# A first expert product by Strassen's seven block products instead of eight, in an fp32r attention and mixture-of-experts kernel

## The chip, the cores and the metric

One core of one Trainium2 chip runs the whole kernel in one launch. The metric is device time of the launch in microseconds (us); the time before is a median of three runs. Engines are written as in the profile: PE is the matrix engine, PEld its weight loads, DVE the vector engine, ACT the scalar engine, POOL GpSimd, SP the engine whose queue issues the DMAs.

## What is computed

An attention over 2 batches of 8 heads feeds a gated layer and then a mixture of four experts. The reference, cut to what the change touches (1152 tokens, model width 512, four experts of width 1024):

```python
def _moe_ref(x, w_a, w_b, w_out):
    a = x @ w_a
    b = x @ w_b
    return a * b @ w_out

def _moe2_ref(x, domain_probs, w1, w2):
    N, D = x.shape
    E = w1.shape[0]
    p = domain_probs / (domain_probs.sum(-1, keepdims=True) + 1e-09)
    out = np.zeros((N, D), dtype=np.float32)
    for e in range(E):
        h = np.maximum(x @ w1[e], 0.0)
        out += p[:, e:e + 1] * (h @ w2[e])
    return out
```

## The kernel before, in words

Every large product is made of three PE products: a number is kept as a high part rounded to fp32r and a low part that is the rest, and high by high, low-data by high-weight and high-data by low-weight are summed in PSUM. `mm3` (line 876) writes this for one output tile of 128 features by 1152 tokens: for each block of 128 in the contracted dimension, three part pairs, and for each of these three matmuls of 384 tokens (line 884), each with a weight load of its own.

There are four stages, one after the other. **Attention** fills the first 281 us. The **gated stage** makes twelve tiles `G[f]` out of `w_a` and `w_b`. The **w_out stage** sums the twelve `G[f]` into four tiles of `X`, one per 128 model features `d`: 12 x 9 = 108 matmuls each, then ACT writes the high part (line 955) and DVE the low part (line 956). `w_out` arrives as float64 and is decoded by `decode64` on ACT, DVE and POOL two half tiles ahead (`w_split`). The **expert stage** goes through four experts. For an expert, `h_chunk` (lines 974 to 985) makes eight feature tiles of `h`: 4 x 9 = 36 matmuls of 384 columns, then relu to a high part on ACT (line 980) and a low part on DVE (line 981). Between them `w_split` splits the next 1024 columns of `w1` or `w2` (ACT line 222, DVE line 223). Then, for nine token tiles of 128, 8 x 3 = 24 matmuls of 512 columns (line 1007) multiply `h` by `w2`, and DVE adds the weighted result to `acc` (lines 1012 and 1016). The first feature tile of the next expert is made before the last token tile. PSUM has two halves of three banks for feature tiles and banks 6 and 7 in turn for token tiles.

All engines run in the order in which the kernel is written, each in its own order, with semaphores between them. Weights are loaded by SP in items of 1 MB into two buffers `stg`; an item's load is issued when an older item has been split.

Of the kernel before, what the change touches and what calls it, by code (L numbers as in the profile page):

```python
# [20 lines left out]
NT = B * SQ  # L21
# [70 lines left out]
def kernel(  # L92
# [16 lines left out]
    wsp = ctx.enter_context(tc.tile_pool(name="wsp", bufs=2))  # L109
# [7 lines left out]
    X = xpool.tile([128, 2, KC, NT], F32R, name="X")  # L117

# [9 lines left out]
    for e in range(E):  # L128
        at = len(items)
        for kind, u in (("w1", 0), ("w1", 1), ("w2", 0), ("w1", 2), ("w2", 1), ("w1", 3), ("w2", 2), ("w2", 3)):  # L130
            splits.append((kind, (e, u), at + u // 2 * 2 + (kind == "w2"), (u % 2) * 1024, 1024))
        items += [src[e, i].bitcast(I32) for i in range(2) for src in (w1, w2)]
# [13 lines left out]
    def decode64(raw, hi, lo, n):  # L146
        parts = []
        for i in range(2):
            cs = slice(i * n // 2, (i + 1) * n // 2)
            v, c, t = (pools["tmp"].tile([128, pools["n"]], F32, tag=f"{x}{i}", name=x)[:, :n // 2] for x in "vct")  # L150
            low, high = raw[:, cs, 0].bitcast(U32), raw[:, cs, 1].bitcast(U32)
            parts.append((low, high, v, v.bitcast(U32), c, c.bitcast(U32), t, hi[:, cs], lo[:, cs]))
# [43 lines left out]
    def w_split():  # L196
        for _ in w_split_steps():
            pass

    def w_split_steps():  # L200
        i = nxt["split"]
        if i >= len(splits):
            return
        nxt["split"] += 1
        kind, idx, item, off, n = splits[i]
        if kind == "w2":
            pool = pools["w2"]
        elif kind == "w1":
            pool = wsp
        else:  # L210
            pool = pools["w3"] if i % 3 == 2 else wsp
        t = pool.tile([128, 2, 1024], F32R, tag="w", name="w")
        s = staged[item]
        if kind in ("ab", "o"):
            raw = s.rearrange("p (n w) -> p n w", w=2)
            for o in range(0, n, 2 * pools["n"]):
                cs = slice(o, min(n, o + 2 * pools["n"]))
                yield from decode64(raw[:, cs, :], t[:, 0, cs], t[:, 1, cs], cs.stop - o)
            last = True
        else:  # L220
            s = s[:, off:off + n].bitcast(F32)
            nc.scalar.activation(out=t[:, 0, :n], in_=s, func=AF.Copy)  # L222
            nc.vector.tensor_tensor(  # L223
                out=t[:, 1, :n], in0=s, in1=t[:, 0, :n].bitcast(F32), op=ALU.subtract
            )
            last = off > 0
        W[kind, idx] = t
        if last:
            del staged[item]
            w_dma()  # L230

    with tc.manual_schedule():
# [11 lines left out]
        pools["tmp"] = att.enter_context(tc.tile_pool(name="tmp", bufs=1))  # L244
# [646 lines left out]

        g_x = ExitStack()
        g_p = g_x.enter_context(tc.tile_pool(name="g", bufs=1))
        a_sp = g_x.enter_context(tc.tile_pool(name="asb", bufs=1))
        pools["n"] = 512
        pools["tmp"] = g_x.enter_context(tc.tile_pool(name="tmp2", bufs=1))
        pools["w3"] = g_x.enter_context(tc.tile_pool(name="w3", bufs=1))
        G = [g_p.tile([128, 2, NT], F32R, name=f"G{f}") for f in range(NF)]
        xs = lambda kc: X[:, :, kc, :]

        def gv(t):
            return t.rearrange("p (n c) -> p n c", c=TOK)
# [4 lines left out]
        def gate(f, groups):  # L907
            asb = a_sp.tile([128, NT], F32, tag="a", name="asb")
# [25 lines left out]
        for f in range(1, NF):  # L934
            if f == STOP:
                g_x.close()
# [9 lines left out]
        for d in range(KC):  # L946
            px2 = psum("ps", 0, NTC, 2)
            for hf in range(2):
                w = W.pop(("o", (d, hf)))
                if (d, hf) != (KC - 1, 0):  # L950
                    w_split()
                hs = range(hf * NF // 2, (hf + 1) * NF // 2)
                mm3(banks(px2), lambda f: w, lambda f: (f % (NF // 2)) * 128, lambda f: G[f],
                    hs, range(NTC), 0, NF - 1)
            nc.scalar.activation(out=gv(X[:, 0, d, :]), in_=px2[:, :, :TOK], func=AF.Copy)
            nc.vector.tensor_tensor(
                out=gv(X[:, 1, d, :]), in0=px2[:, :, :TOK],
                in1=gv(X[:, 0, d, :].bitcast(F32)), op=ALU.subtract,
            )
        g_x.close()  # L960

        pools["w2"] = ctx.enter_context(tc.tile_pool(name="w2p", bufs=4))
        h_p = ctx.enter_context(tc.tile_pool(name="h", bufs=9))
        acc_p = ctx.enter_context(tc.tile_pool(name="acc", bufs=1))
        acc = acc_p.tile([128, NTT, DM], F32, name="acc")

        nc.sync.dma_start(out=p_sb, in_=probs)
        nc.vector.tensor_reduce(out=p_sum, in_=p_sb, axis=AX.X, op=ALU.add)
        nc.vector.tensor_scalar(out=p_sum, in0=p_sum, scalar1=1e-9, scalar2=None, op0=ALU.add)
        nc.vector.reciprocal(out=p_rec, in_=p_sum)  # L970
        for e in range(E):
            nc.vector.tensor_tensor(out=p_n[:, :, e], in0=p_sb[:, :, e], in1=p_rec, op=ALU.mult)

        def h_chunk(e, f):
            w = W["w1", (e, f // 2)]
            ph = psum("ps", 0, NTC, 2)
            mm3(banks(ph), lambda kc: w, lambda kc: ((f % 2) * KC + kc) * 128, xs,
                range(KC), range(NTC), 0, KC - 1)
            hs = h_p.tile([128, 2, NT], F32R, tag="h", name="hs")
            nc.scalar.activation(out=gv(hs[:, 0, :]), in_=ph[:, :, :TOK], func=AF.Relu)  # L980
            nc.vector.scalar_tensor_tensor(  # L981
                out=gv(hs[:, 1, :]), in0=ph[:, :, :TOK], scalar=0.0,
                in1=gv(hs[:, 0, :].bitcast(F32)), op0=ALU.max, op1=ALU.subtract,
            )
            return hs

        hs = [None] * NFE
        for e in range(E):
            for f in range(NFE):
                if hs[f] is None:  # L990
                    hs[f] = h_chunk(e, f)
                if f < 7:
                    w_split()
            cur, hs = hs, [None] * NFE
            w2s = [W.pop(("w2", (e, u))) for u in range(4)]
            for tt in range(NTT):
                if tt == 1 and e + 1 < E:
                    w_split()
                if tt == NTT - 1 and e + 1 < E:
                    hs[0] = h_chunk(e + 1, 0)  # L1000
                po = psum("po", 6, 1, 2)[:, 0, :]
                ts = slice(tt * 128, (tt + 1) * 128)
                for f in range(NFE):
# [7 lines left out]
                if e == 0:  # L1011
                    nc.vector.tensor_scalar(
                        out=acc[:, tt, :], in0=po, scalar1=p_n[:, tt, 0:1], scalar2=None, op0=ALU.mult
                    )
                else:
                    nc.vector.scalar_tensor_tensor(  # L1016
                        out=acc[:, tt, :], in0=po, scalar=p_n[:, tt, e:e + 1], in1=acc[:, tt, :],
                        op0=ALU.mult, op1=ALU.add,
                    )
                if e == E - 1:  # L1020
                    nc.sync.dma_start(out=out[ts, :], in_=acc[:, tt, :])
# [43 lines left out]
```

## Time and profile before

| what | us |
|---|---|
| median of three runs (906.33, 906.46, 908.34) | 906.46 |
| span of the profiled execution, first to last instruction | 907.1 |
| PE busy | 896.2 (99%) |
| DVE busy | 459.4 (51%) |
| ACT busy | 270.8 (30%) |
| POOL busy | 71.6 (8%) |

The profiled execution is known by its span, 907.1 us; its own time on the clock of the runs is not marked among the three, and the span lies 0.6 us above their median. The profile counts a PE matmul from its start to its modelled end, so matmuls overlap and the mean duration of one is longer than the step from one to the next. The step is what a stage costs, and it is had from a merged row of the chain of waits (time over count) or from the starts of rows in the timeline.

### The profile page before, as it was taken

To read this page: it belongs to the slowest core of one execution; us is meant where nothing else is said; L and a number is where in the kernel's file an instruction comes from. 1 tells how busy PE (TensorE), PEld (TensorE's weight loads), DVE (VectorE), ACT (ScalarE), POOL (GpSimd) and SP (SyncE) were. 2 spreads that over 40 slices of the span, in tenths; PEclk is the share of its full clock that TensorE was granted. 3 is DMA by queue.
4 is the path that set the end of the run, shared out by engine and by line. 5 is a ranking of instruction groups with operands and counts; after the bars stand their busy time and mean duration, and the time that the engine had idled before them with its cause. 6 is when DMAs were issued, how large, how long until landed. Compare 5 with 4: busy or idle time off the path is not lost.

```text
span 907.1 us, 11505 instructions
## 1 busy us (share of the span) xinstructions
PE 896.2 (99%) x4709; PEld 818.5 (90%) x4709; DVE 459.4 (51%) x793; ACT 270.8 (30%) x395; POOL 71.6 (8%) x42
## 2 busy tenths in 40 slices
PE   8999999999999999999999999999999999999998
PEld 6787888888889999999999999889988998899986
DVE  5875766776605888988784243114321242114311
ACT  4444455545453333333321222002300221003200
POOL 6000000000000222222221000000000000000000
PEclk9999999999999999999999999999999999999999
DMA  7567676766440222212212112001300121011011
GB/s 181 128 152 197 154 187 162 180 158 151 120 111 1 94 93 93 85 49 79 91 70 94 47 54 86 1 0 47 135 5 1 47 94 47 1 43 51 4 54 47
DMA packets 49385, 76.99 MB, mean 85 GB/s; under 512 B 32496, under 2 KB 36084, under 8 KB 45748
## 3 DMA queue, kind: packets, MB, share of 16 engines
q1 hardware_dynamic: 49332, 76.25, 29.7%
q8 instruction: 37, 0.61, 0.3%
q14 instruction: 16, 0.13, 0.0%
HBM read 51.96 MB, written 2.39 MB: 60 GB/s over the span
## 4 chain that ended last, share of the span: by engine, by line
PE 93%; DVE 3%; DMA 2%; SPq 1%; ACT 1%; issue 0%; DVEq 0%; ACTq 0%
PE PS L884 44%; PE PS L1007 22%; PE PS L543 14%; PE PS L418 5%; PE PS L528 4%; PE PS L533 4%; PE PS L508 1%; DMA kq<-in_kq_dram 1%; SPq L390 1%; DMA QH<-QH 0%; DVE R L872 0%; SPq L144 0%; DVE v L168 0%; DVE m L433 0%; PE PS L499 0%
## 5 line engine op out<-in xcount | busy, mean ns | idle before, releaser
L884 PE MATMUL PS<-X,w 128*128 128x384 f32 x2016 | 351.7, 334 | 0.6 <-ACT asb L910 0.5
L884 PEld LDWEIGHTS PS<-X,w 128*128 128x128 f32 x2016 | 349.7, 188 | 1.8 <-ACT asb L910 1.3
L1007 PE MATMUL PS<-w,hs 128*128 128x512 f32 x864 | 197.3, 389 | 0.0
L1007 PEld LDWEIGHTS PS<-w,hs 128*128 128x128 f32 x864 | 162.1, 188 | 33.4
L543 PE MATMUL PS<-e,VF 128*128 128x288 f32 x540 | 150.6, 410 | 0.7 <-ACT U L564 0.3
L433 DVE TENSOR_REDUCE m<-PS 128x1 f32<-128x384 f32 (+1 forms) x213 | 112.0, 553 | 61.2 <-PE PS L418 57.6
L980 ACT ACTIVATE hs<-PS 128x1152 fp32r<-128x1152 f32 x32 | 36.3, 1135 | 281.3 <-PE PS L884 281.3
L538 ACT ACTIVATE e<-PS 128x576 f32<-128x576 f32 x135 | 84.5, 649 | 113.8 <-PE PS L533 113.1
L543 PEld LDWEIGHTS PS<-e,VF 128*128 128x128 f32 x540 | 98.8, 190 | 20.3 <-ACT U L564 0.9
L981 DVE SCALAR_TENSOR_TENSOR hs<-PS,hs 128x1152 fp32r<-128x1152 f32 x32 | 43.4, 1357 | 134.3 <-ACT hs L980 134.3
L188 POOL TENSOR_TENSOR t<-v,w 128x512 f32<-128x512 f32 (+2 forms) x22 | 56.4, 2564 | 408.1 <-ACT w L178 408.1
L1016 DVE SCALAR_TENSOR_TENSOR acc<-PS,p_n,acc 128x512 f32<-128x512 f32 x27 | 20.3, 751 | 115.7 <-PE PS L1007 115.7
L418 PE MATMUL PS<-kh,QB 128*128 128x384 f32 x189 | 73.1, 427 | 2.9 <-DVE m L433 2.6
L884 PE MATMUL PS<-G,w 128*128 128x384 f32 x432 | 75.0, 334 | 0.0
L884 PEld LDWEIGHTS PS<-G,w 128*128 128x128 f32 x432 | 74.9, 188 | 0.0
L528 PE MATMUL PS<-QH,A 128*128 128x288 f32 x270 | 65.5, 324 | 0.0
L533 PE MATMUL PS<-QL,B 128*128 128x288 f32 x270 | 57.6, 295 | 0.0
L528 PEld LDWEIGHTS PS<-QH,A 128*128 128x128 f32 x270 | 48.3, 190 | 5.7
L418 PEld LDWEIGHTS PS<-kh,QB 128*128 128x128 f32 x189 | 35.1, 190 | 11.4 <-DVE m L433 5.7
L533 PEld LDWEIGHTS PS<-QL,B 128*128 128x128 f32 x270 | 43.6, 189 | 0.0
L223 DVE TENSOR_TENSOR w<-stg,w 128x1024 fp32r<-128x1024 f32 x32 | 38.9, 1215 | 8.1 <-ACT w L222 8.1
L193 DVE TENSOR_TENSOR w<-t,c 128x512 fp32r<-128x512 f32 (+2 forms) x44 | 39.3, 931 | 1.0
(84 smaller groups left out, 482.6 us busy)
## 6 DMA issues: line engine op xcount, KB each, us to landing
stg<-in_w_dram SPq DMA_DIRECT2D x16, 1024.0 KB
stg<-in_wab_dram SPq DMA_DIRECT2D x12, 1024.0 KB
stg<-in_wout_dram SPq DMA_DIRECT2D x8, 768.0 KB
VF<-in_vo_dram SPq DMA_DIRECT2D x16, 288.0 KB
A<-kl SPq DMA_DIRECT2D x15, 288.0 KB
q<-in_kq_dram SPq DMA_DIRECT2D x7, 576.0 KB
kq<-in_kq_dram SPq DMA_DIRECT2D x21, 192.0 KB
A<-kh SPq DMA_DIRECT2D x14, 288.0 KB
```

The source lines that it names most:

```text
L188: nc.gpsimd.tensor_tensor(out=t, in0=v, in1=h.bitcast(F32), op=ALU.subtract)
L193: nc.vector.tensor_tensor(out=l, in0=t, in1=c, op=ALU.add)
L223: nc.vector.tensor_tensor(out=t[:, 1, :n], in0=s, in1=t[:, 0, :n].bitcast(F32), op=ALU.subtract)
L418: nc.tensor.matmul(out=out[:lhs.shape[1]], lhsT=lhs, rhs=rhs, start=True, stop=True)
L433: nc.vector.tensor_reduce(out=max_slot(h, qi)[:, r:r + 1], in_=mx[:n_q(h, qi)], axis=AX.X, op=ALU.max)
L528: nc.tensor.matmul(out=st[:, c, :HQ], lhsT=At[i][:, ks], rhs=QHt[i][:, c * HQ:(c + 1) * HQ], start=True, stop=False,)
L533: nc.tensor.matmul(out=st[:, c, :HQ], lhsT=Bt[i][:, ks], rhs=QLt[i][:, c * HQ:(c + 1) * HQ], start=False, stop=True,)
L538: nc.scalar.activation(out=e, in_=st[:, :, :HQ], func=AF.Exp, scale=1.0 / 16.0)
L543: nc.tensor.matmul(out=PS[:, c, :HQ], lhsT=VFt[h % 2][:, t, :], rhs=e[:, c, :], start=(t == 0), stop=(t == KT - 1),)
L884: nc.tensor.matmul(out=ps[n], lhsT=wt(kc)[:, wi, w0:w0 + 128], rhs=src(kc)[:, xi, n * TOK:(n + 1) * TOK], start=(kc == first and i == 0), ...
L981: nc.vector.scalar_tensor_tensor(out=gv(hs[:, 1, :]), in0=ph[:, :, :TOK], scalar=0.0, in1=gv(hs[:, 0, :].bitcast(F32)), op0=ALU.max, op1=A ...
L1007: nc.tensor.matmul(out=po, lhsT=cur[f][:, hi, ts], rhs=wv[:, wi, cs], start=(f == 0 and i == 0), stop=(f == NFE - 1 and i == 2),)
```

## The change

The first expert product is rewritten with the form of Strassen's identity that needs seven block products. The contracted dimension and the features are taken in blocks of 128 as 2 x 2 blocks: a pair `p` of feature tiles (f0, f1) is one side, the four blocks of 128 model features the other, and the tokens are cut into halves T1 and T2 of 576. For each of 16 pairs, `h_pair` runs seven products (`product`), each over two blocks of 128, three part pairs and two matmuls of 288 tokens: 12 matmuls, into one of three pairs of PSUM banks. The sums of weight blocks (S1 to S4) are made per pair on DVE (`prep_w1`). The sums of token blocks (T1 to T4) do not depend on the expert and are made once, in the w_out stage, out of PSUM; that stage's last tile (d = 3) is for this cut into two token halves (`o_last`) of 72 matmuls of 288 columns. The seven results are added up by DVE in SBUF tiles `v1` to `v4`, and relu then makes high and low parts out of these. The product with `w2` runs once per two pairs, that is eight times over nine token tiles of 12 matmuls, where before it ran four times over nine tiles of 24; DVE adds into `acc` 72 times, before 36. Of the token tiles those of T2 come first. Buffers of the gated stage (`GT`) are reused for sums, weights and `h`. The decode in the gated stage keeps its difference in the buffer of its input.

The diff, cut to its core:

```diff
-    wsp = ctx.enter_context(tc.tile_pool(name="wsp", bufs=2))
+    wsp = ctx.enter_context(tc.tile_pool(name="wsp", bufs=1))
...
+        def tmp_g(i):
+            v, c = (tmp4[:, 2 * i + j, :] for j in range(2))
+            return v, c, v
...
+        def prep_w1(p, tmp, then=True):
+            k, q = divmod(p, 2)
+            s = f32(staged[len(splits) + 2 * k][:, q * 1024:(q + 1) * 1024])
+            a11, a12, a21, a22 = (s[:, i * 256:(i + 1) * 256] for i in range(4))
...
+            tt(tmp[:, 0], a11, a21, ALU.subtract)
+            tt(a21, a21, a22, ALU.add)
+            tt(tmp[:, 1], a21, a11, ALU.subtract)
+            act(t[:, :, 0], s)
+            yield
+            tt(t[:, :, 1], s, f32(t[:, :, 0]), ALU.subtract)
+            tt(a12, a12, tmp[:, 1], ALU.subtract)
+            yield
+            s23, s4 = pair_sets.get(p, sets[q])
+            hl = s23.rearrange("p h (j n) -> p h j n", j=2)
+            act(hl[:, 0], tmp)
+            act(s4[:, 0], a12)
+            tt(hl[:, 1], tmp, f32(hl[:, 0]), ALU.subtract)
+            tt(s4[:, 1], a12, f32(s4[:, 0]), ALU.subtract)
...
+        def prep_w2(p):
...
+            act(t[:, :, 0], s)
+            tt(t[:, :, 1], s, f32(t[:, :, 0]), ALU.subtract)
...
+        o_last(1)
+        tt(hv(b12[1]), pd[1], hv(b12[1]), ALU.subtract)
+        tt(hv(t1[1]), pd[1], hv(t1[1]), ALU.subtract)
+        split(opT["T2"][0], t2)
+        split(opT["T2"][1], t1[1])
+        split(opT["T3"][0], b12[0])
+        split(opT["T3"][1], b12[1])
+        split_ps(X[:, :, 3, T2], pd[1])
+        run(prep_w1(1, w_tmp))
+        o_last(0)
+        tt(hv(t1[1]), pd[0], hv(t1[1]), ALU.subtract)
+        split_ps(X[:, :, 3, T1], pd[0])
+        split(opT["T4"][0], t4)
+        split(opT["T4"][1], t1[1])
...
+                for j, (wi, xi) in enumerate(((0, 0), (0, 1), (1, 0))):
+                    for n in range(2):
+                        nc.tensor.matmul(
+                            out=q[:, n], lhsT=lhs[:, wi, i * 128:(i + 1) * 128],
+                            rhs=rhs[:, xi, n * HC:(n + 1) * HC],
+                            start=(i == 0 and j == 0), stop=(i == 1 and j == 2),
+                        )
+            return q
...
+        def h_pair(p, work):
+            f0, f1 = 2 * (p % 2), 2 * (p % 2) + 1
+            v1, v2, v3, v4 = (hv(v) for v in vs)
+            act(v1, product(p, "A11", "B11"))
+            tt(v2, v1, product(p, "S2", "T2"), ALU.add)
+            tt(v3, v2, product(p, "S3", "T3"), ALU.add)
+            next(work, None)
+            q = product(p, "S1", "T1")
+            tt(v2, v2, q, ALU.add)
+            tt(v4, v3, q, ALU.add)
+            relu_hi(f1, T2, v4)
+            tt(v1, v1, product(p, "A12", "B21"), ALU.add)
+            relu_hi(f0, T1, v1)
+            relu_lo(f1, T2, v4)
+            tt(v2, v2, product(p, "S4", "B22"), ALU.add)
+            relu_hi(f0, T2, v2)
+            relu_lo(f0, T1, v1)
+            next(work, None)
+            relu_lo(f0, T2, v2)
+            tt(v3, v3, product(p, "A22", "T4"), ALU.add)
+            relu_hi(f1, T1, v3)
+            relu_lo(f1, T1, v3)
+            next(work, None)
...
-                for f in range(NFE):
-                    wv = w2s[f // 2]
-                    cs = slice((f % 2) * DM, (f % 2 + 1) * DM)
+                for f in range(4):
...
-                            out=po, lhsT=cur[f][:, hi, ts], rhs=wv[:, wi, cs],
-                            start=(f == 0 and i == 0), stop=(f == NFE - 1 and i == 2),
+                            out=po, lhsT=hs[f][:, hi, ts], rhs=w2s[f // 2][:, f % 2, wi],
+                            start=(f == 0 and i == 0), stop=(f == 3 and i == 2),
```

The built program has 1344 matmuls of `product`, 144 of `o_last`, 1188 of 384 columns in the gated stage and the first three tiles of the w_out stage, and 864 of 512 columns; attention is the same, instruction for instruction. Before, there are 2448 of 384 columns (1152 of them in `h_chunk`, 432 in the w_out stage) and 864 of 512. How the order of the instructions moved is shown at three places.

DVE in the expert stage of before, between two feature tiles (`hs` is a feature tile, `w` a split weight tile):

```order
L981 SCALAR_TENSOR_TENSOR hs_4974<-PS_108,hs_4974 128x1152
L223 TENSOR_TENSOR w_4977<-stg_4625,w_4977 128x1024
L981 SCALAR_TENSOR_TENSOR hs_5016<-PS_108,hs_5016 128x1152
L223 TENSOR_TENSOR w_5019<-stg_4936,w_5019 128x1024
L981 SCALAR_TENSOR_TENSOR hs_5058<-PS_108,hs_5058 128x1152
```

And DVE of the change in the second pair of a group, where every odd pair has the low part of a `w2` tile (row 3) in its chain:

```order
L948 TENSOR_TENSOR v2_4275<-v1_4274,PS_110 128x576
L948 TENSOR_TENSOR v3_4276<-v2_4275,PS_110 128x576
L948 TENSOR_TENSOR GT_2391<-stg_4772,GT_2391 128x2x512
L948 TENSOR_TENSOR v2_4275<-v2_4275,PS_110 128x576
L948 TENSOR_TENSOR v4_4277<-v3_4276,PS_110 128x576
L948 TENSOR_TENSOR v1_4274<-v1_4274,PS_110 128x576
L1137 SCALAR_TENSOR_TENSOR GT_2391<-v4_4277,GT_2391 128x576
L948 TENSOR_TENSOR v2_4275<-v2_4275,PS_110 128x576
L1137 SCALAR_TENSOR_TENSOR GT_2391<-v1_4274,GT_2391 128x576
L1137 SCALAR_TENSOR_TENSOR GT_2391<-v2_4275,GT_2391 128x576
L948 TENSOR_TENSOR v3_4276<-v3_4276,PS_110 128x576
L1137 SCALAR_TENSOR_TENSOR GT_2391<-v3_4276,GT_2391 128x576
```

One DVE pass over a finished feature tile has become eleven passes over half rows for two tiles, seven of which read PSUM and free it.

PE at the end of a group's products and in the first token tile behind them, of the change (a wait in brackets names the engine waited for; the `GT` on the left of a 512-column row is `h`):

```order
L1126 MATMUL PS_110<-X_73,GT_2391 128x288 [waits DVE_49]
L1126 MATMUL PS_110<-X_73,GT_2391 128x288 x11
L1126 MATMUL PS_110<-GT_2391 128x288 [waits DVE_49]
L1126 MATMUL PS_110<-GT_2391 128x288 x11
L1198 MATMUL PS_110<-GT_2391 128x512 x6
L1198 MATMUL PS_110<-GT_2391 128x512 [waits Activation_49]
L1198 MATMUL PS_110<-GT_2391 128x512
L1198 MATMUL PS_110<-GT_2391 128x512 [waits DVE_49]
L1198 MATMUL PS_110<-GT_2391 128x512 x15
```

The token tile's seventh matmul waits for ACT and its ninth for DVE: these read the T2 half of the odd pair's f0, the last one of that half to be finished.

DVE at the change's last tile of the w_out stage (`asb`, `x0` and `x1` hold token sums; the rows begin when the T2 half has been summed in PSUM):

```order
L948 TENSOR_TENSOR asb_2403<-PS_110,asb_2403 128x576
L948 TENSOR_TENSOR x0_2404<-PS_110,x0_2404 128x576
L948 TENSOR_TENSOR GT_2391<-x1_2405,GT_2391 128x576
L948 TENSOR_TENSOR GT_2391<-x0_2404,GT_2391 128x576
L948 TENSOR_TENSOR GT_2391<-asb_2403,GT_2391 128x576 x2
L948 TENSOR_TENSOR X_73<-PS_110,X_73 128x576
L948 TENSOR_TENSOR w_tmp_4083<-stg_3935 128x256
L948 TENSOR_TENSOR stg_3935<-stg_3935 128x256
L948 TENSOR_TENSOR w_tmp_4083<-stg_3935 128x256
L948 TENSOR_TENSOR GT_2391<-stg_3935,GT_2391 128x2x512
L948 TENSOR_TENSOR stg_3935<-stg_3935,w_tmp_4083 128x256
L948 TENSOR_TENSOR GT_2391<-w_tmp_4083,GT_2391 128x512
```

Before, one row (line 956) stands in this place; now the token sums and the second pair's weight sums are made there, beside the T1 half's matmuls on PE.

## Rows read from the trace of the kernel before

**Rows 1.** The page's span, PE's busy time, and the granted clock in 40 slices.

```profile
span 907.1 us, 11505 instructions
PE 896.2 (99%) x4709; PEld 818.5 (90%) x4709; DVE 459.4 (51%) x793; ACT 270.8 (30%) x395; POOL 71.6 (8%) x42
...
PEclk9999999999999999999999999999999999999999
```

**Rows 2.** Busy time by stretch: us, each engine's busy us (instructions), granted clock, DMA.

```profile
400.00:450.00 50.00, 50.00 (x290) 50.00 (x289) 43.38 (x81) 15.87 (x26) 13.34 (x5) 1.00 0.21 66
...
550.00:600.00 50.00, 50.00 (x232) 42.61 (x231) 10.23 (x11) 4.16 (x4) 0.00 (x0) 1.00 0.06 22
```

**Rows 3.** Chain that ended last: start us, us, engine, line, instructions merged; expert stage.

```profile
557.30 43.56 PE PS L1007 x192
...
612.61 43.70 PE PS L884 x252
...
854.34 49.02 PE PS L1007 x216
```

**Rows 4.** PE's timeline in attention: start us, us from first start to last end.

```profile
183.78 0.42 PE L533 MATMUL PS<-QL,B 128*128 128x288 f32 x2
184.04 0.42 PE L528 MATMUL PS<-QH,A 128*128 128x288 f32 x2
184.31 0.43 PE L533 MATMUL PS<-QL,B 128*128 128x288 f32 x2
184.57 0.41 PE L543 MATMUL PS<-e,VF 128*128 128x288 f32 x1
```

**Rows 5.** Line 884 by instruction: duration ns min/median/max, first and last start, forms.

```profile
L884 PEld LDWEIGHTS PS<-G,w x432: 187/188/188, 432.2 to 506.9; 128*128 128x128 f32 x144
L884 PE MATMUL PS<-G,w x432: 334/334/334, 432.3 to 507.0; 128*128 128x384 f32 x144
```

**Rows 6.** The weight loads' timeline in the same piece of attention.

```profile
183.65 0.32 PEld L533 LDWEIGHTS PS<-QL,B 128*128 128x128 f32 x2
183.91 0.32 PEld L528 LDWEIGHTS PS<-QH,A 128*128 128x128 f32 x2
184.18 0.32 PEld L533 LDWEIGHTS PS<-QL,B 128*128 128x128 f32 x2
```

**Rows 7.** Groups of DVE and ACT instructions: busy us, mean ns, idle before and its releaser.

```profile
L981 DVE SCALAR_TENSOR_TENSOR hs<-PS,hs 128x1152 fp32r<-128x1152 f32 x32 | 43.4, 1357 | 134.3 <-ACT hs L980 134.3
L223 DVE TENSOR_TENSOR w<-stg,w 128x1024 fp32r<-128x1024 f32 x32 | 38.9, 1215 | 8.1 <-ACT w L222 8.1
L1016 DVE SCALAR_TENSOR_TENSOR acc<-PS,p_n,acc 128x512 f32<-128x512 f32 x27 | 20.3, 751 | 115.7 <-PE PS L1007 115.7
L184 DVE SCALAR_TENSOR_TENSOR c<-stg,c 128x512 f32<-128x512 uint32 x20 | 12.8, 682 | 0.0
L340 DVE TENSOR_TENSOR qs<-q 128x576 f32<-128x576 f32 x7 | 5.3, 753 | 0.0
L597 DVE TENSOR_TENSOR U<-U,R 128x288 f32<-128x288 f32 x16 | 7.2, 452 | 5.7 <-DMA R<-rd 5.5
L538 ACT ACTIVATE e<-PS 128x576 f32<-128x576 f32 x135 | 84.5, 649 | 113.8 <-PE PS L533 113.1
L222 ACT ACTIVATE w<-stg 128x1024 fp32r<-128x1024 f32 x32 | 33.7, 1053 | 8.4 <-PE PS L884 8.4
```

**Rows 8.** Timeline of DVE and ACT in the w_out stage, third tile.

```profile
472.41 0.62 DVE L157 TENSOR_SCALAR c<-c 128x384 f32<-128x384 f32 x2
...
485.01 1.65 DVE L193 TENSOR_TENSOR w<-t,c 128x384 fp32r<-128x384 f32 x2
...
488.69 1.14 ACT L955 ACTIVATE X<-PS 128x1152 fp32r<-128x1152 f32 x1 [5.14 <-PE PS L884]
```

**Rows 9.** Busy time in the stretch in which one weight item of 1 MB lands.

```profile
517.30:523.00 5.70, 5.70 (x35) 5.70 (x34) 2.00 (x3) 2.08 (x2) 0.00 (x0) 1.00 0.48 184
```

**Rows 10.** Timeline of the end: the last addition on DVE and the last store.

```profile
903.38 0.75 DVE L1016 SCALAR_TENSOR_TENSOR acc<-PS,p_n,acc 128x512 f32<-128x512 f32 x1 [4.69 <-PE PS L1007]
904.15 0.33 SPq L1021 DMA_DIRECT2D out_dram<-acc  x1
```

More of the change, by code (lines that the diff above doesn't have):

```diff
@@ L117 @@
     X = xpool.tile([128, 2, KC, NT], F32R, name="X")
+    WA = [wsp.tile([128, 2, 1024], F32R, name=f"WA{i}") for i in range(2)]
     items = []
@@ L128 @@
     for e in range(E):
[L129 to L132, printed above, removed]
+        for i in range(2):
+            items += [w1[e, i].bitcast(I32), w2[e, i].bitcast(I32)]
     nxt = {"dma": 0, "split": 0}
@@ L205, in w_split_steps @@
         kind, idx, item, off, n = splits[i]
[L206 to L226, printed above, removed]
+        t = WA[i % 3]
+        raw = staged[item].rearrange("p (n w) -> p n w", w=2)
+        for o in range(0, n, 2 * pools["n"]):
+            cs = slice(o, min(n, o + 2 * pools["n"]))
+            yield from decode64(raw[:, cs, :], t[:, 0, cs], t[:, 1, cs], cs.stop - o)
         W[kind, idx] = t
-        if last:
-            del staged[item]
-            w_dma()
+        del staged[item]
+        w_dma()
     with tc.manual_schedule():
@@ L944, with act, tt, f32 @@
             gate(f, [(pa[:, :, :TOK], pb[:, :, :TOK], 0, NT)])
-        for d in range(KC):
+        HT = NT // 2
+        HC = HT // 2
+        SP = HT - TOK
+        T1, T2 = slice(0, HT), slice(HT, NT)
+        def act(out, in_, func=AF.Copy):
+            nc.scalar.activation(out=out, in_=in_, func=func)
+        def tt(out, in0, in1, op):
+            nc.vector.tensor_tensor(out=out, in0=in0, in1=in1, op=op)
+        def f32(t):
+            return t.bitcast(F32)
+        def split(t, v):
+            act(t[:, 0], v)
+            tt(t[:, 1], v, f32(t[:, 0]), ALU.subtract)
@@ new lines, in o_w @@
+        def o_w(d, hf):
+            w = W.pop(("o", (d, hf)))
+            if d < KC - 1:
+                w_split()
+            return w
+        b12 = [asb[:, i * HT:(i + 1) * HT] for i in range(2)]
+        t1 = [b12[1], t1b]
+        opT = {n: [] for n in ("T2", "T3", "T4")}
+        for i in range(2):
+            opT["T2"].append(GT[:, i, :, T2])
+            opT["T3"].append(GT[:, 2 + i, :, T2])
+            opT["T4"].append(GT[:, i, :, T1])
+        sets = [
+            (GT[:, 4, :, HT:HT + 512], GT[:, 5, :, HT:HT + 256]),
+            (GT[:, 2, :, 0:512], GT[:, 3, :, 0:256]),
+        ]
@@ new lines, in prep_w2, with run @@
+        def prep_w2(p):
+            k, q = divmod(p, 2)
+            s = f32(staged[len(splits) + 2 * k + 1][:, q * 1024:(q + 1) * 1024])
+            s = s.rearrange("p (j n) -> p j n", j=2)
+            t = W["w2", p] = slot_of(4 * k + 2 + q)
+            act(t[:, :, 0], s)
+            tt(t[:, :, 1], s, f32(t[:, :, 0]), ALU.subtract)
+            if q == 1:
+                del staged[len(splits) + 2 * k + 1]
+                w_dma()
+        def run(steps):
+            for _ in steps:
+                pass
@@ L955 @@
[L955 to L958, printed above, removed]
-            )
[L960 to L985, printed above, removed]
@@ L987 @@
-        hs = [None] * NFE
-        for e in range(E):
-            for f in range(NFE):
[L990 to L1000, printed above, removed]
+                    fs, range(NTC), 0, NF - 1)
@@ new lines, with o_last @@
+        d_x.close()
+        s_p = g_x.enter_context(tc.tile_pool(name="s0", bufs=1))
+        pair_sets[0] = [s_p.tile([128, 2, n], F32R, name=f"s{n}") for n in (512, 256)]
+        w_tmp = s_p.tile([128, 512], F32, name="w_tmp")
+        run(prep_w1(0, w_tmp))
+        w = [o_w(KC - 1, hf) for hf in range(2)]
+        pd = [PS[:, 6:8, :HC], PS[:, 4:6, :HC]]
+        def o_last(half):
+            at = half * HT
+            for f in range(NF):
+                for i, (wi, xi) in enumerate(((0, 0), (0, 1), (1, 0))):
+                    for n in range(2):
+                        nc.tensor.matmul(
+                            out=pd[half][:, n],
+                            lhsT=w[f // (NF // 2)][:, wi, (f % (NF // 2)) * 128:(f % (NF // 2) + 1) * 128],
+                            rhs=G[f][:, xi, at + n * HC:at + (n + 1) * HC],
+                            start=(f == 0 and i == 0), stop=(f == NF - 1 and i == 2),
+                        )
@@ new lines @@
+        run(prep_w1(1, w_tmp))
[4 more added lines that the diff above has]
+        split(opT["T4"][1], t1[1])
+        a_x.close()
+        v_p = ctx.enter_context(tc.tile_pool(name="v", bufs=1, side="right"))
+        s_tmp, *vs = (v_p.tile([128, n], F32, name=f"v{i}") for i, n in enumerate((512, HT, HT, HT, HT)))
+        turn["q"] = 0
+        Q = [PS[:, 2 * i:2 * i + 2, :HC] for i in range(3)]
@@ new lines, in product @@
+        def product(p, a, b):
+            q = Q[turn["q"] % 3]
+            turn["q"] += 1
+            t = W["w1", p]
+            s23, s4 = pair_sets.get(p, sets[p % 2])
+            lhs = {
+                "A11": t[:, 0, :, :256], "A12": t[:, 0, :, 256:], "S1": t[:, 1, :, :256], "A22": t[:, 1, :, 256:],
+                "S3": s23[:, :, 0:256], "S2": s23[:, :, 256:512], "S4": s4,
+            }[a]
+            for i in range(2):
+                rhs = {
+                    "B11": X[:, :, 2 * i, T1], "T1": X[:, :, 2 * i, T2],
+                    "B21": X[:, :, 2 * i + 1, T1], "B22": X[:, :, 2 * i + 1, T2],
+                }[b] if b not in opT else opT[b][i]
+                for j, (wi, xi) in enumerate(((0, 0), (0, 1), (1, 0))):
+                    for n in range(2):
+                        nc.tensor.matmul(
+                            out=q[:, n], lhsT=lhs[:, wi, i * 128:(i + 1) * 128],
+                            rhs=rhs[:, xi, n * HC:(n + 1) * HC],
+                            start=(i == 0 and j == 0), stop=(i == 1 and j == 2),
+                        )
+            return q
@@ new lines, in prep2, with ahead @@
+        def prep2(*ps):
+            for p in ps:
+                if p is not None:
+                    prep_w2(p)
+                yield
+        NP = E * 4
+        for k in range(NP // 2):
+            e = k // 2
+            for p in (2 * k, 2 * k + 1):
+                if k == 0:
+                    h_pair(p, prep2(p) if p else prep2(None, None, 0))
+                    if p == 0:
+                        g_x.close()
+                        a_p = ctx.enter_context(tc.tile_pool(name="acc", bufs=1))
+                        acc = a_p.tile([128, NTT, DM], F32, name="acc")
+                else:
+                    h_pair(p, prep2(p) if p % 2 else iter(()))
+            work = iter(())
+            if k + 1 < NP // 2:
+                def ahead(k=k + 1):
+                    yield from prep_w1(2 * k, s_tmp)
+                    yield from prep_w1(2 * k + 1, s_tmp)
+                    prep_w2(2 * k)
+                    yield
+                work = ahead()
+            w2s = [W.pop(("w2", 2 * k + q)) for q in range(2)]
+            for tt_i in (5, 6, 7, 8, 0, 1, 2, 3, 4):
@@ L1016 @@
                     nc.vector.scalar_tensor_tensor(
-                        out=acc[:, tt, :], in0=po, scalar=p_n[:, tt, e:e + 1], in1=acc[:, tt, :],
+                        out=acc[:, tt_i, :], in0=po, scalar=p_n[:, tt_i, e:e + 1], in1=acc[:, tt_i, :],
                         op0=ALU.mult, op1=ALU.add,
                     )
-                if e == E - 1:
-                    nc.sync.dma_start(out=out[ts, :], in_=acc[:, tt, :])
+                next(work, None)
+                if k == NP // 2 - 1:
+                    nc.sync.dma_start(out=out[ts, :], in_=acc[:, tt_i, :])
+            run(work)
 def kernel(**inputs):
```

94 lines of the change are left out of this document (75 added, 19 removed).

## The prediction

> **What bounds the kernel now.** I read the page's busy times and clock row first [rows 1]: PE is busy 896.2 of 907.1 us, at a granted clock that stands at 9 or more tenths in every slice (the 2.4 GHz level). So the kernel costs what its matmuls cost, and another engine matters only where it makes PE wait. The busy times by stretch [rows 2] say the same for the two stages that change: PE 50.00 of 50.00 us in the w_out stage and in the expert stage, while DVE has 10.23 of 50 us in a stretch of the expert stage. Then the chain of waits [rows 3] gives PE's step from one matmul to the next, since it merges long runs without a gap: 43.70 us for 252 matmuls of 384 columns is 173.4 ns each; 43.56 us for 192 and 49.02 us for 216 of 512 columns is 226.9 ns each. The w_out stage has the same step (432 matmuls start from 432.3 to 507.0 us, 74.7 / 431 = 173.3 ns [rows 5]). From 384 to 512 columns the step grows by 53.5 ns, 0.418 ns a column.
>
> The change replaces matmuls of 384 columns by fewer columns in more matmuls of 288. So the forecast rests on the step of a 288-column matmul, and then on whether DVE, which gets the sums, keeps out of PE's way.
>
> **The step at 288 columns.** Attention has such matmuls in the same fp32r form: six in a row, in two PSUM banks in turn as in the change, start from 183.78 to 184.57 us [rows 4]: 0.79 / 6 = 131.7 ns. The long rows, carried down by 0.418 ns a column, give 173.4 - 96 x 0.418 = 133.3 ns. I take 132.5, between the two; both ends stay in the range. What attention cannot show is a long run, since its runs are cut by slower matmuls. Each matmul has a weight load of 187 to 188 ns [rows 5]. These overlap: in the w_out stage one starts every 173 ns, and between the 288-column matmuls of attention the starts of two pairs lie 183.91 and 184.18 us [rows 6], 135 ns a load, so nothing there holds a load back to 173 ns.
>
> A rule speaks against the change here. The Trainium skill, Perfetto Trace Analysis, section "Identifying the Most-Contended Engine", tells the reader to judge the matrix engine by the busy share of weight loads, not of matmuls, and its section "Matmuls" says that larger matmuls are more efficient. By that reading the w_out stage, where PEld is busy all of 50.00 us [rows 2], would be bound by its loads, and more loads with fewer columns would be slower; the trace agrees that the share is full, but not that a load needs the whole step, since rows 6 have loads that start closer together. It is kept as a rival below.
>
> **The sum on PE.** In the expert stage go 32 x 36 = 1152 matmuls x 173.4 ns = 199.8 us; 16 x 7 x 12 = 1344 x 132.5 ns = 178.1 us come: -21.7 us. The product with `w2` keeps its 864 matmuls of 512 columns, 196.0 us before and after; that they come in eight rounds of nine tiles instead of four costs PE nothing by itself, since the step between matmuls of different lines is the same merged run [rows 3]. In the w_out stage the last tile's 108 x 173.4 = 18.7 us become 144 x 132.5 = 19.1 us: +0.4 us. Attention and the gated stage are unchanged; the decode that now works in place keeps its order on DVE, ACT and POOL, so I cost it at nothing. The weight items are as many and as large as before; one lands within 5.7 us (184 GB/s x 5.7 us = 1.05 MB [rows 9]), and a group of 46.8 us (14 products of 1.59, nine tiles of 2.72) needs two.
>
> **What DVE gets, and where it hides.** A pass over 576 columns in fp32 takes 0.753 us, one over 1024 1.215, over 512 0.682, over 288 0.452 (so no more for 256) [rows 7]. From PSUM the price per column is the same: 1152 in 1.357 us. Per pair: seven additions and four low parts, 11 x 0.753 = 8.3 us, and 1.2 us for `w2` in odd pairs, beside 7 x 1.59 = 11.1 us of PE. Beside nine token tiles, 24.5 us: nine additions to `acc` at 0.751 = 6.8, two `prep_w1` at most 5 x 0.452 + 0.682 + 1.215 = 4.2 each, one `w2` low part 1.2: 16.4 us. ACT has 5 x 0.65 us per pair and 1.05 us per hidden weight part [rows 7]. So by amount all of it fits.
>
> By latency, the tight place is the end of an odd pair. From the pair's start in us, with 0.2 for a matmul's tail and a semaphore: PE's products end at 1.59, 3.18, 4.77, 6.36, 7.95, 9.54 and 11.13. DVE adds `v2` from 3.4, `v3` from 5.0 to 5.7, the `w2` part to 6.95, `v2`, `v4` and `v1` to 9.2, the low part of f1/T2 to 10.0, `v2` to 10.7, the low part of f0/T1 to 11.5, of f0/T2 to 12.25. PE's first token tile starts at 11.13 and reads that last part in its ninth matmul, at 11.13 + 8 x 0.227 = 12.95. That leaves 0.7 us. T1 is not read until the fifth tile, 10 us later. A PSUM pair is reused three products, 4.8 us, after it was begun, and is read within some 2 us of its end. I allow 0.5 us for all eight groups, against 2 us if every DVE pass were 0.1 us longer.
>
> In the w_out stage, DVE's decode in the third tile runs from 472.41 to 486.66 us, the tile's matmuls to 488.69 [rows 8]. The sums after the second tile put 3 to 4 us ahead of it, so it ends near 490.5; the half that is late, the last tile's second weight half, is first read 36 x 0.1325 = 4.8 us after 488.7. The third tile's sums (2.5 us) and `prep_w1(0)` (4.2) then run to about 497.8, beside `o_last(1)`, 9.5 us to 498.2. Seven passes and `prep_w1(1)` (5.3 + 4.2 and some waits on ACT) run to 508.4, beside `o_last(0)` to 507.7, and four more to 511.4. The first three products read nothing of these last four; the fourth, at 512.5, needs the PSUM pair that ACT empties at about 511.8. It fits with less than 1 us left: I allow 0.5 us.
>
> **Sum.** -21.7 + 0.4 + 0.5 + 0.5 = -20.3 us on the profiled span of 907.1: 886.8. The end is as before (last addition at 903.38, then the store [rows 10]). The median stands 0.6 us under that span: 886.2, so **886 us**.
>
> **Rivals.**
>
> *Weight loads set the step; slower.* If in a long run a load cannot start sooner than 173.4 ns after the last, the full PEld of rows 2 is the bound: 1344 x 173.4 = 233.0 us in place of 199.8, and 144 x 173.4 = 25.0 in place of 18.7: +39.5 us, 946. It decides from a step of (199.8 + 18.7) / 1488 = 147 ns on; above that the change is slower. For it: PEld is full, and no long run of short matmuls is in the trace. Against it: 131.7 ns over six matmuls, and the even 0.418 ns a column between two steps of which only one has PEld full (42.61 of 50 us at 512 columns [rows 2]). Chance 0.06.
>
> *DVE becomes the bound.* Its work in the expert stage goes from about a fifth of the time to 16 x (8.3 + 4.2 + 1.2) + 72 x 0.751 = 273 of 374 us. If passes with PSUM as one operand and two more waits each take 0.2 us longer, a pair needs 11 x 0.95 + 1.4 = 11.9 us against 11.1, and each group loses about 2.5 us: 8 x 2.5 = 20 us, 906, no change; half of that is 895. For it: 176 short passes in place of 32 long ones. Against it: 1152 columns from PSUM cost 1.357 us, no more than the columns explain. Chance 0.10, 0.03 of it within no change.
>
> *Token sums come late.* If DVE's chain in the w_out stage misses its cover by one `prep_w1`, the products start 4.2 us later, once: 890. Chance 0.04.
>
> **How the numbers follow.** The forecast has the other 0.80. Its own range is 882 (131 ns, no waits at all, 1 us for the rounding of rows) to 889 (133.5 ns, 1.5 us, and DVE passes 0.1 us longer, 2 us). Up to 894 the range takes in the late token sums and about half of the DVE rival. The three runs lie 2.0 us apart; about 0.3%, 2.7 us, is what a measurement of this kernel can tell from no change. Faster: 0.80 + 0.07 + 0.04 = 0.91; same 0.03; slower 0.06.
>
> **What would show it.** Right: in the profile of the changed kernel the 288-column matmuls of `product` step by 131 to 134 ns in merged runs, the 512-column ones still by 227, PE busy 99%, DVE busy near 630 us, and PE's idle time before `product` and before the token tiles under 2 us in all. Wrong: a step near 173 ns (loads), PE idle before a token tile's ninth matmul or before a product with DVE as its releaser (DVE), or one gap of microseconds near 510 us (token sums).

## The result, and the profile after

| | before | after |
|---|---|---|
| median of the runs, us | 906.45 (906.33 to 908.34) | 887.33 (885.46 to 887.72) |
| span of the profiled execution, us | 907.1 | 885.9 |
| PE busy, us | 896.2 | 874.6 |
| DVE busy, us | 459.4 | 620.6 |
| ACT busy, us | 270.8 | 311.2 |

The changed kernel takes 0.9778 of the time before (95% interval 0.9764 to 0.9792, about 18.9 to 21.4 us less); the medians lie 19.1 us apart. The forecast was 886 us, 882 to 894, and the time lies in that range. The page of the changed kernel begins:

```profile
span 885.9 us, 12401 instructions
...
PE 874.6 (99%) x4937; PEld 796.9 (90%) x4937; DVE 620.6 (70%) x1093; ACT 311.2 (35%) x490; POOL 68.7 (8%) x42
```

PE is as full as before, 99%, with less to do. The chain of waits of the changed kernel has the stages in merged runs (start us, us, engine, line, instructions; lines 1075 `o_last`, 1126 `product`, 1198 the product with `w2`):

```profile
487.85 19.19 PE PS L1075 x144
507.04 22.40 PE PS L1126 x168
529.44 24.50 PE PS L1198 x108
553.95 22.38 PE PS L1126 x168
576.33 24.50 PE PS L1198 x108
...
857.65 24.52 PE PS L1198 x108
```

The expert stage runs from 507.04 to 882.17 us without a break: 375.1 us. Before, it ran from about 507.4 (the last matmul of the w_out stage starts at 507.0 and takes 0.33 [rows 5]) to 854.34 + 49.02 = 903.36 [rows 3], 396.0 us. So 20.9 us were saved there. The step of a 288-column matmul is 22.38 / 168 = 133.2 ns, that of a 512-column one 24.50 / 108 = 226.9, as before. `o_last` takes 19.19 us where 108 x 173.4 = 18.7 stood. So the two changed stages are 20.4 us shorter. The rest of the difference of the spans, 0.8 us, is in the stages ahead, which the change leaves alone but for the place of one difference in the decode; in the profiles of the runs below, which all have these stages as the changed kernel has them, their length varies by over 2 us.

DVE's new passes, by group (busy us, mean ns, idle time before them and its releaser), and a stretch of two rounds:

```profile
L948 DVE TENSOR_TENSOR v<-v,PS 128x576 f32<-128x576 f32 x112 | 82.7, 752 | 42.0 <-PE PS L1126 39.8 <-ACT v L945 0.8 <-ACT WA L945 0.8
L1137 DVE SCALAR_TENSOR_TENSOR GT<-v,GT 128x576 fp32r<-128x576 f32 x64 | 48.4, 756 | 13.7 <-ACT GT L945 12.0
L1207 DVE SCALAR_TENSOR_TENSOR acc<-PS,p_n,acc 128x512 f32<-128x512 f32 x63 | 47.3, 750 | 58.1 <-PE PS L1198 58.1
```

```profile
650.00:700.00 50.00, 50.00 (x301) 45.77 (x301) 33.51 (x49) 12.64 (x19) 0.00 (x0) 1.00 0.12 43
```

A pass over 576 columns with PSUM as an operand takes 752 ns, what rows of before gave for 576 columns in SBUF [rows 7]. DVE is busy 33.51 of 50 us in the expert stage (10.23 in a stretch before [rows 2]) and waits for PE, while PE is busy for 50.00.

The tight place is the end of an odd pair. From the timeline of the changed kernel (DVE's two low parts of f0, then the first token tile on PE), and from its start of the expert stage (ACT empties the first product's PSUM, then the fourth product and the fifth):

```profile
716.10 1.59 DVE L1137 SCALAR_TENSOR_TENSOR GT<-v,GT 128x576 fp32r<-128x576 f32 x2
```

```profile
716.83 3.13 PE L1198 MATMUL PS<-WA,GT 128*128 128x512 f32 x13
```

```profile
510.75 0.65 ACT L945 ACTIVATE v<-PS 128x576 f32<-128x576 f32 x1 [1.07 <-DVE GT L948]
```

```profile
511.68 3.36 PE L1126 MATMUL PS<-X,WA 128*128 128x288 f32 x24
```

The low part of f0 in T2 ends at 717.69; its reader, the ninth matmul, starts at 716.83 + 8 x 0.2269 = 718.65 (718.67 by its own record): 0.96 to 0.97 us to spare. At the start of the stage the spare time is 511.68 - 511.40 = 0.28 us. ACT's copy there is not held up by ACT's own work: ACT is idle for 1.07 us before it and is released by DVE's last pass over a token sum. By the kernel's code the copy's target `v1` lies in the memory that the token sums give back (`a_x.close()`), so it cannot be written before they have been read; this is read from the code, and no run tests it.

### The profile page after: what moved, and what is told of

Read it like the earlier page. It is cut to its first block, busy times and chain, and to the rows that moved or that the text cites. A ratio compares the mean times of both kernels' runs of the same rounds, so it can differ in the third digit from the quotient of the medians.

```text
span 885.9 us, 12401 instructions
## 1 busy us (share of the span) xinstructions
PE 874.6 (99%) x4937; PEld 796.9 (90%) x4937; DVE 620.6 (70%) x1093; ACT 311.2 (35%) x490; POOL 68.7 (8%) x42
## 4 chain that ended last, share of the span: by engine, by line
PE 66%; issue 0%; ACT 0%; DVE 0%; ACTq 0%
PE PS L1198 22%; PE PS L867 22%; PE PS L1126 20%; PE PS L1075 2%; DVE acc L1207 0%; ACT WA L177 0%; ACT tmp L153 0%; ACT asb L904 0%; ACTq L908 0%
## 5 line engine op out<-in xcount | busy, mean ns | idle before, releaser
L867 PE MATMUL PS<-X,WA 128*128 128x384 f32 x864 | 150.7, 334 | 0.7 <-issue 0.6
L867 PEld LDWEIGHTS PS<-X,WA 128*128 128x128 f32 x864 | 149.7, 188 | 1.5 <-issue 0.9
L1198 PE MATMUL PS<-GT 128*128 128x512 f32 x594 | 139.8, 389 | 0.0
L1198 PEld LDWEIGHTS PS<-GT 128*128 128x128 f32 x594 | 111.1, 188 | 22.8
L948 DVE TENSOR_TENSOR v<-v,PS 128x576 f32<-128x576 f32 x112 | 82.7, 752 | 42.0 <-PE PS L1126 39.8
L945 ACT ACTIVATE GT<-v 128x576 fp32r<-128x576 f32 (+1 forms) x78 | 52.5, 674 | 118.5 <-DVE v L948 118.2
L1126 PE MATMUL PS<-X,GT 128*128 128x288 f32 x468 | 66.1, 296 | 0.0
L1198 PE MATMUL PS<-WA,GT 128*128 128x512 f32 x270 | 65.8, 389 | 0.0
L1126 PE MATMUL PS<-GT 128*128 128x288 f32 x456 | 64.5, 296 | 0.0
L1126 PEld LDWEIGHTS PS<-X,GT 128*128 128x128 f32 x468 | 63.8, 189 | 0.2
L1126 PEld LDWEIGHTS PS<-GT 128*128 128x128 f32 x456 | 62.1, 189 | 0.0
```

Of the source, the lines that this page charges most:

```text
L867: nc.tensor.matmul(out=ps[n], lhsT=wt(kc)[:, wi, w0:w0 + 128], rhs=src(kc)[:, xi, n * TOK:(n + 1) * TOK], start=(kc == first and i == 0), ...
L945: nc.scalar.activation(out=out, in_=in_, func=func)
L948: nc.vector.tensor_tensor(out=out, in0=in0, in1=in1, op=op)
L1126: nc.tensor.matmul(out=q[:, n], lhsT=lhs[:, wi, i * 128:(i + 1) * 128], rhs=rhs[:, xi, n * HC:(n + 1) * HC], start=(i == 0 and j == 0), st ...
L1198: nc.tensor.matmul(out=po, lhsT=hs[f][:, hi, ts], rhs=w2s[f // 2][:, f % 2, wi], start=(f == 0 and i == 0), stop=(f == 3 and i == 2),)
```

## The experiments

The lines quoted are of each run's own profile. Runs with one time are single executions with a profile; the stages are compared by their rows, since the spans of one kernel lie up to 2 us apart.

**e1_eight: the identity undone, the new cut kept.** Four results per pair, each from its four plain block products; the sums of weights are gone and the even tiles' T2 half holds plain tokens:

```diff
-                split(X[:, :, d, T2], t1[i])
+                split(X[:, :, d, T2], b12[i])
...
-            act(v1, product(p, "A11", "B11"))
-            tt(v2, v1, product(p, "S2", "T2"), ALU.add)
...
+            for f, half in ((1, 1), (0, 1), (1, 0), (0, 0)):
+                q = product(p, f, half)
+                ts = (T1, T2)[half]
+                relu_hi(f0 + f, ts, q)
+                relu_lo(f0 + f, ts, q)
```

> The changed kernel with one part undone: each half of tokens and each feature tile is summed from its four block products of the plain product (16 pairs x 4 results x 24 = 1536 matmuls of 288 columns instead of 1344), relu goes straight from PSUM, weight sums are not made and DVE has 8 passes fewer per pair; cut of the tokens, order, token sums and the rounds with w2 stay. Theory (the gain is the block product left out, at the step of 133.3 ns that the changed kernel shows): +192 x 133.3 = +25.6 us, span 911.5, time near 913, about 0.7% slower than before, PE idle as little as now. Rival (the gain is from the new order of stages or from relu and w2 in smaller rounds): within 5 us of the changed kernel's 887. Rival (the plain product is as quick in the new cut as it was): 906.

Measured: 911.14 us, 1.0059 of before (95% interval 1.0041 to 1.0077). Its chain of waits, first rounds:

```profile
504.71 25.60 PE PS L1110 x192
530.30 24.50 PE PS L1168 x108
554.81 25.58 PE PS L1110 x192
```

A round of two pairs has 192 matmuls in 25.58 us, the same 133.2 ns, and is 3.2 us longer than the changed kernel's 22.38; eight rounds make 25.6 us. By the medians it is 23.8 us slower than the changed kernel (the stages ahead of `o_last` were 2 us quicker in this profile). So the whole gain is the block product left out. The cut into 288 columns alone costs time: with eight products the kernel is about 5 us slower than before.

**e2_cols256 and e3_cols192: how far the step falls with the columns.**

```diff
-                            out=q[:, n], lhsT=lhs[:, wi, i * 128:(i + 1) * 128],
-                            rhs=rhs[:, xi, n * HC:(n + 1) * HC],
+                            out=q[:, n, :256], lhsT=lhs[:, wi, i * 128:(i + 1) * 128],
+                            rhs=rhs[:, xi, n * HC:n * HC + 256],
```

> The changed kernel whose block products compute only 256 of each 288 columns (32 of 288 tokens of each part are left out of the expert product; DVE and ACT still pass over 576). Theory (a matmul costs its columns plus a fixed 13.4 ns, as from 288 to 512): step 119.9 ns, and the expert stage loses 1344 x 13.4 = 18 us where DVE allows it: span 868 to 872. Rival (every fourth step of 140 ns in the changed kernel is the sign that instructions or weight loads do not come faster than one pair in 133 ns): step stays 131 to 134 ns, span 884 to 887.

> The same with 192 of each 288 columns. Theory: step 93 ns within a product, and DVE becomes the bound in the products: a pair has 8.3 to 9.5 us of DVE and 84 x 0.093 = 7.8 us of PE, so PE waits for DVE before products and before token tiles, and the pairs cost some 9 us instead of 11.2: span 850 to 856. Rival (floor of instructions or weight loads): step 131 to 134 ns, span 884 to 887.

Measured: 864.47 us and 859.26 us. A round of products in the chain of waits, with 256 columns and then with 192:

```profile
594.43 19.60 PE PS L1126 x168
```

```profile
593.50 18.74 PE PS L1126 x168
```

The steps are 116.7 and 111.5 ns. At 256 columns the step is 3.2 ns under the theory's 119.9; why the part above the columns shrinks there stays open. At 192 it is neither 93 nor 133: with a third fewer columns than 288 it is only 22 ns less, and PE has no wait for DVE in these rounds. So there is a floor, but at 111 ns, below the 133 of the change.

**e9_cols192_w64: what the floor is.** 192 columns, and 64 of the 128 columns of each weight block:

```diff
-                            out=q[:, n], lhsT=lhs[:, wi, i * 128:(i + 1) * 128],
-                            rhs=rhs[:, xi, n * HC:(n + 1) * HC],
+                            out=q[:64, n, :192], lhsT=lhs[:, wi, i * 128:i * 128 + 64],
+                            rhs=rhs[:, xi, n * HC:n * HC + 192],
```

> The changed kernel with 192 of each 288 columns, and with weight blocks of 64 of their 128 columns (a third of the tokens and half of the features are left out of the expert product; as many matmuls and weight loads as with 192 columns alone, where the step stood at 111 ns). Theory (the 111 ns are the time to load 128 weight columns; the Trainium skill, TensorE: Matmul & The Clock Gate, section on LDWEIGHTS, gives a load time that goes with the number of columns, 107 ns for 128): the step falls to 85 to 95 ns, and PE then waits for DVE in the products. Rival (the 111 ns are the supply of instructions, two per matmul): the step stays at 111 ns.

Measured: 855.32 us. PE's timeline in a round (start us, us, count; in brackets the idle time and its releaser):

```profile
602.38 1.23 PE L1126 MATMUL PS<-GT,WA 128*64 128x192 f32 x12
603.45 1.23 PE L1126 MATMUL PS<-X,WA 128*64 128x192 f32 x12
604.52 1.23 PE L1126 MATMUL PS<-GT 128*64 128x192 f32 x12
606.27 1.28 PE L1126 MATMUL PS<-GT 128*64 128x192 f32 x12 [0.53 <-DVE v L948]
```

Twelve matmuls start every 1.07 us, 89 ns each, with as many instructions as at 111 ns. So the floor is not the supply of instructions. But halving the weight columns halves the rows of each result as well, so the shorter step alone does not say whether the load or the matmul set the floor. The records of the loads help: line 1126 with 128 weight columns (e3), then with 64 (ns min/median/max):

```profile
L1126 PEld LDWEIGHTS PS<-X,GT x468: 186/192/192, 514.3 to 827.3; 128*128 128x128 f32 x156
```

```profile
L1126 PEld LDWEIGHTS PS<-X,GT x468: 132/134/138, 516.9 to 821.9; 128*64 128x64 f32 x156
```

With half of the columns a load is 58 ns shorter, and in the expert stage of e5 below no load of 128 columns starts less than 107 ns after the one before it. So the floor is the load of 128 weight columns. PE now also waits for DVE: this is the DVE rival, at a product of 1.07 us.

**e4_together: the cover of the token sums taken away.** The last w_out tile's halves are summed in turn, feature by feature:

```diff
-        def o_last(half):
-            at = half * HT
-            for f in range(NF):
+        def o_both():
+            for f, half in ((f, half) for f in range(NF) for half in (1, 0)):
+                at = half * HT
...
-        o_last(1)
+        o_both()
...
-        o_last(0)
```

> The changed kernel with the last w_out tile's two token halves summed feature by feature in turn, so that both are finished at the same time and the token sums and the second pair's weight sums lose their cover of 9.6 us of matmuls. Theory: PE waits about 1.5 us before the second product (T2 is split only then) and about 3.5 us before the fifth (the T1 half of the last tile follows the second pair's weight sums on DVE), 4 to 6 us in all, span 890 to 892. Rival (the token sums are hidden by something else, or are not on the path): span 885 to 887, no wait of PE near 507 us.

Measured: 895.41 us, 8.1 us over the changed kernel's median. From the start of the last w_out tile to the end of the chain's last PE row it is 404.3 us, against 882.17 - 487.85 = 394.3, so by the rows the cover was worth 10.0 us:

```profile
485.47 18.41 PE PS L1075 x138
...
865.26 24.52 PE PS L1197 x108
```

PE's waits in `product` (line 1125 here), longest in total first, busy time by stretch (the figure behind the fifth bracket is the granted clock), and ACT's timeline at the long wait:

```profile
PE PS L1125 <- ACT v L945: 6.9, 1, 6.9
...
PE PS L1125 <- DVE X L948: 1.1, 1, 1.1
```

```profile
507.00:510.50 3.50, 2.40 (x18) 2.17 (x17) 3.08 (x6) 1.57 (x3) 0.00 (x0) 1.00 0.00 0
510.50:517.70 7.20, 0.31 (x3) 0.08 (x1) 5.35 (x9) 3.67 (x7) 0.00 (x0) 0.76 0.43 146
517.70:521.10 3.40, 3.39 (x14) 3.39 (x15) 1.60 (x3) 0.00 (x0) 0.00 (x0) 0.51 0.00 0
521.10:524.00 2.90, 2.90 (x24) 2.90 (x23) 2.63 (x4) 1.21 (x2) 0.00 (x0) 1.00 0.00 0
```

```profile
514.69 1.25 ACT L945 ACTIVATE GT<-x 128x576 fp32r<-128x576 f32 x2
...
517.01 0.65 ACT L945 ACTIVATE v<-PS 128x576 f32<-128x576 f32 x1 [1.07 <-DVE GT L948]
```

The sums are on the path as soon as their cover is gone. The places were not the ones expected. PE waits 1.1 us before the third product, whose PSUM still holds the T2 half of the last tile, and 6.9 us before the fourth, whose PSUM still holds the first product's result until ACT has copied it to `v1`. That copy stands behind all conversions of token and weight sums in ACT's order, and then waits for DVE too: ACT is done with the conversions at 515.94 and idle for 1.07 us, until DVE has read the last token sum, as in the changed kernel. After the idle time the granted clock is 0.51, the 1.2 GHz level, over the next 14 matmuls (240 ns each), which loses another 1.5 us.

**e7_pass1 and e8_pass3: DVE's spare time.**

```diff
+            if p % 2:
+                for _ in range(1):
+                    tt(s_tmp, vs[3][:, :512], vs[3][:, :512], ALU.add)
             relu_lo(f0, T2, v2)
```

> The changed kernel with one more DVE pass over 512 columns (0.68 us, its result is not read) in each odd pair, just before the low part of f0 in T2. Theory (in the changed kernel that part is finished 0.97 us before the ninth matmul of the first token tile starts, so DVE has that much to spare): no wait, span as the changed kernel, 884 to 886. Rival (DVE is on the path): 0.68 us in each of eight groups, +5.4 us.

> The same with three more passes, 2.04 us. Theory: 2.04 - 0.97 = 1.07 us of wait before the ninth matmul in each of eight groups, +8.6 us, span 893 to 895, PE idle there with DVE as its releaser. Rival (DVE on the path already): +16 us. Rival (much more to spare than the one place shows): no change.

Measured: 885.65 and 894.12 us, on the same chip. With one more pass, a round is as in the changed kernel (first fence, its chain of waits); with three, PE waits in every group (second fence, its waits: us in total, times, longest; third fence, its chain of waits):

```profile
786.23 22.38 PE PS L1126 x168
808.61 24.50 PE PS L1201 x108
```

```profile
PE PS L1201 <- DVE GT L1137: 6.6, 8, 0.9
```

```profile
485.18 19.19 PE PS L1075 x144
...
865.58 23.00 PE PS L1201 x100
```

0.68 us more costs nothing. 2.04 us more cost 8.5 us by the two times; by the rows, from the start of the last w_out tile to the last matmul, 403.4 against 394.3, it is 9.1, or 1.1 in each of eight groups, where 2.04 - 0.97 = 1.07. (The 6.6 of the waits is less because a wait is counted only from the modelled end of the matmul before it.) The spare time read from the trace is all there is at this place.

**e5_384_192 and e6_320_256: a try for a better cut.** The 576 tokens in unequal parts, over two banks in one piece:

```diff
-        Q = [PS[:, 2 * i:2 * i + 2, :HC] for i in range(3)]
+        parts = (slice(0, WIDE), slice(WIDE, HT))
+        Q = [over(2 * i) for i in range(3)]
...
-                            rhs=rhs[:, xi, n * HC:(n + 1) * HC],
+                            rhs=rhs[:, xi, cs],
```

> The changed kernel with the 576 tokens of each block product (and of each half of the last w_out tile) cut into 384 and 192 columns instead of 288 and 288; the result lies in one piece over two PSUM banks, so that DVE and ACT pass over it as before. The runs with 256 and 192 columns showed that the cost above the columns shrinks with them (13.3 ns at 288, 10 at 256, 5 at 192 as long as loads are ahead, 111 ns a matmul at least when they are not). Theory (the floor of 111 ns holds for the mean of the pair, the 384 gives the next load its time): 173.4 + 85 to 90 = 259 to 263 ns a pair instead of 266.6, 744 pairs: 3 to 5.5 us less, 882 to 884. Rival (the cost above the columns is fixed at 13.4 ns, or the 192 pays its 111 ns each time): 266.8 or 284.5 ns a pair, 887 or 900.

> The same with 320 and 256 columns. Theory: 146.7 + 117 = 263.5 ns a pair, 744 x 3.1 = 2.3 us less than the changed kernel, 885. Rival (fixed cost): 266.8, 887.

Measured: 900.54 us, 0.9941 of before (0.9927 to 0.9955), and 886.47, 0.9779 (0.9766 to 0.9792). A late round of products in each one's chain of waits:

```profile
797.51 23.87 PE PS L1133 x168
```

```profile
788.18 22.39 PE PS L1133 x168
```

384 and 192 take 23.87 / 84 = 284.2 ns, as if the 192 paid the 111 ns of the floor although its neighbour has time over. In the records of this round the loads start 108 to 109 and 175 to 177 ns apart in turn: the time over is not used to start a load sooner. 320 and 256 take 266.5, as 288 and 288 do. Both follow the rival, and no better version came of it: e6 cannot be told from the changed kernel.

## Why the prediction was right

*The step at 288 columns.* Taken as 132.5 ns, between a short run's 131.7 and 133.3 from the long rows; measured 133.2 over runs of 168. The upper end was right, and the short run of attention flattered by 1.5 ns: in the records of `product` three steps of 130 to 132 ns are followed by one of 140, and the six steps in attention have no such step.

*The sum on PE.* -21.7 + 0.4 us forecast; measured -20.9 in the expert stage and +0.5 in the last w_out tile. The 0.7 ns by which the step was taken too short are 1.0 us over 1488 matmuls. They were made up by the 1 us allowed for waits, of which nothing was used: that -20.3 us in all came so near the measured -20.4 is in part luck. e1 shows that the gain is the left-out product.

*Weight loads as the bound.* Rejected for the right reason as to the place (a load every 135 ns in attention), and the point from which the change turns slower, 147 ns, was 14 ns away. But the rival had a true core that the trace of before could not show: loads do set the step, at 111 ns (e3, e9). By the Trainium skill, TensorE: Matmul & The Clock Gate, section "LDWEIGHTS (loading the stationary operand)", a load takes its number of columns divided by 1.2, in ns; for 128 columns that makes an estimate of 107 ns. e3's step of 111.5 agrees within 5 ns, and the closest load starts in e5, 107 ns apart, agree with it too. The Trainium skill's reading by the busy share of weight loads, in Perfetto Trace Analysis, section "Identifying the Most-Contended Engine", would have had the change some 40 us slower by the prediction's working. That share was full at a step of 173 ns [rows 2], and in the changed kernel it is full at 133 (a round of products; PEld is the second figure with a count):

```profile
553.95:576.33 22.38, 22.38 (x169) 22.38 (x169) 15.65 (x22) 6.95 (x10) 0.00 (x0) 1.00 0.13 48
```

So a full share does not tell whether the loads bind.

*DVE hides.* Each pass cost what was taken (752 against 753 ns). The spare time at the first token tile was put at 0.7 us and is 0.97; e7 and e8 show that it is real and how soon it is gone.

*Token sums hide.* They do, with 0.28 us over instead of the 0.7 worked out. The prediction had the copy that frees the fourth product's PSUM done at 511.8, too early for a copy of 0.65 us that begins behind DVE's last pass at 511.4, and in the trace it does begin behind that pass. So DVE's chain ends the wait, and this dependence on the token sums' memory is a link that the prediction does not name. e4 prices the cover at 10.0 us by the rows, more than the 4.2 of the rival, which knew only of a DVE chain late by one `prep_w1`.

*The median.* The forecast put the median 0.6 us under the span. After the change the profiled run took 887.72 us for a span of 885.9, and the median lies 1.4 us above the span. The span came out 0.9 us lower than forecast (886.8), the median 1.1 higher. In all four runs of the changed kernel the time is 1.8 to 1.9 us above the run's own span, and in a later run of the kernel before, 906.76 us with a span of 905.0, it is so too. By that the profile of before came from an execution of some 908.9 us, no shorter than the slowest of the three runs, and the 0.6 was an accident of that profile.

## What to carry to other kernels

Where PE is full, price a change in matmuls by their steps, from long merged runs, and include the fixed part: here 13 to 14 ns above the columns at 2.4 GHz, from 288 to 512, so that a cut from 384 to 288 costs 2.4% a column (133.2 / 288 against 173.4 / 384) before it saves anything. Then look for the instruction that is last in the shortest cover, on every engine whose order it shares, and count what is left in tenths of a microsecond: here 0.97 and 0.28 us carry a gain of 20. Before cutting further, find the floor: by an estimate from the steps measured at 288, 256 and 192 columns and the 0.418 ns a column, it is reached near 240 columns; no run was made there. At 192, with a load of 128 weight columns before each matmul, the step was 111.5 ns where the columns alone would have made 93.

## What the runs showed of the hardware

The step in fp32r is 226.9 ns at 512 columns, 173.4 at 384, 133.2 at 288, 116.7 at 256 and 111.5 at 192 with a load of 128 weight columns before every matmul, and 89 at 192 with 64 weight columns. In e5's expert stage no load of 128 weight columns started less than 107 ns after the last, and the floor does not average out over neighbours: a 384 beside a 192 takes 284 ns, not the 259 to 263 of that theory. In e4 PE stood idle for 6.9 us; the granted clock was then 0.51, the 1.2 GHz level, while PE ran 14 matmuls, and 1.00 again behind them.
